# Three half blocks of the fifth strip taken ahead of the third strip's last part, in a gated SSM and MLP kernel

## The chip, the cores and the metric

The kernel runs on one core of a Trainium2 chip. The metric is device microseconds (us) of one execution, lower is better.

PE is TensorE (matmuls), PEld its weight loads, DVE is VectorE, ACT is ScalarE, SP issues most transfers. PSUM is the memory that takes PE's results, in banks. L267 is line 267 of the kernel; behind the edit the line numbers of the changed kernel are two higher. In views of the profile, `<-` in brackets names what ended an engine's wait, and "issue" is time in which the engine waited for nothing that the profile shows.

## The reference, cut to what matters

```python
x = A_x                                        # [1, 2048, 640]
g = sigmoid((x * gate_w).sum(-1, keepdims=True))
a = A_ref(x, ...)      # diagonal complex recurrence over 2048 tokens, 640 states
b = gelu(x @ w1 + b1) @ w2 + b2                # 640 -> 1728 -> 640, tanh gelu
return g * a + (1 - g) * b
```

The kernel takes the tokens in four chunks of 512. The change touches only the start: the first 768 columns of `x @ w1` for the first chunk.

## The kernel before

The first chunk's `x` comes as rows of tokens and is transposed on PE (a matmul with the identity, L233), one part of 128 tokens at a time, and copied from PSUM into `xT` by ACT or DVE. The 640 input columns are five blocks of 128 ("strips", `kd` = 0 to 4). Six banks of PSUM (`kf` = 0 to 5) collect `x @ w1` for six blocks of 128 output columns; all take their matmuls from line 267. The lines that matter, shortened:

```python
FA = 6; KD = 5; KA = 2; P = 128; CH = 512; HT = 256

def ff1_mm(p, c, kf, kd, t0=0, t1=CH, first=None, last=KD - 1):   # L267
    ...
    nc.tensor.matmul(p[:, t0:t1], lhsT=w, rhs=xT[c][:, kd, t0:t1], ...)

def strip(kd, t0, t1, first, f0=0, f1=FA):     # strip kd, tokens t0 to t1, for banks f0 to f1
    for kf in range(f0, f1):
        ff1_mm(banks[kf], 0, kf, kd, t0, t1, first, 3)

def part(kd, a):                               # one strip, 128 tokens: six matmuls of 128 columns
    strip(kd, a * P, (a + 1) * P, kd == 0)

def turn_rest(a, t, *parts):                   # transpose strips 2..4 of tokens part a into one bank t
    for k in range(KA, KD):
        turn(t, (k - KA) * P, a, k)            # L233
    for engine, k0, k1 in parts:               # copies out of that bank, in this order
        turned(engine, t, (k0 - KA) * P, a, k0, k1)   # DVE L240, ACT L242

# ... strips 0 and 1, the first parts turned ...
turn_rest(2, bank(), (nc.scalar, KA, KD))
part(2, 0)
nc.vector.tensor_tensor(out=u, ...)            # [128, 345] f32, for the sine tables (L381)
turn_rest(3, pA, (nc.scalar, KA + 1, KD), (nc.vector, KA, KA + 1))
...
part(2, 1)
part(2, 2)
part(2, 3)                                     # needs DVE's copy of turn_rest(3)
... # sine tables on ACT
for kf in range(FA):
    if kf == 3:
        nc.tensor.matmul(pA[:, 0:NB], lhsT=prmB[:], rhs=ident[:, 0:NB], ...)   # biases turned, L393
        ...
    for kd in (4, 3):
        ff1_mm(banks[kf], 0, kf, kd, 0, CH, False, 3)        # 512 columns
for kf in range(FA):
    ff1_act(banks[kf], 0, kf)                  # Gelu out of the banks, L272
# ... second group of w1 (w1b), third (w1c), then the recurrence's input (BT_re, L546) ...
```

Of the kernel before, what the change touches and what calls it, by code (L numbers as in the profile page):

```python
# [20 lines left out]
CH = 512  # L21
NCH = T // CH
KD = D // P
# [6 lines left out]
HT = H * P  # L30
# [11 lines left out]
def kernel(  # L42
# [32 lines left out]
    def bank(dtype=F32):  # L75
        return ps.tile([P, CH * 4 // (4 if dtype == F32 else 2)], dtype, name="bank")
# [140 lines left out]
    def pe(cols):  # L217
        ck.pe += cols / 2400.0 + 0.002
# [45 lines left out]
    def ff1_mm(p, c, kf, kd, t0=0, t1=CH, first=None, last=KD - 1):  # L264
        w, f0 = (w1a, 0) if kf < FA else (w1b, FA) if kf < FB else (w1c, FB)
        w = w[kd][:, (kf - f0) * P:(kf - f0 + 1) * P]
        nc.tensor.matmul(p[:, t0:t1], lhsT=w, rhs=xT[c][:, kd, t0:t1],  # L267
                         start=(kd == 0) if first is None else first, stop=(kd == last), skip_group_check=first is not None)
        pe(t1 - t0)
# [53 lines left out]
    banks = [bank() for _ in range(FA)]  # L323

    def strip(kd, t0, t1, first, f0=0, f1=FA):
        for kf in range(f0, f1):
            ff1_mm(banks[kf], 0, kf, kd, t0, t1, first, 3)
# [26 lines left out]
    def part(kd, a):  # L354
        strip(kd, a * P, (a + 1) * P, kd == 0)
# [28 lines left out]
    nc.vector.tensor_tensor(out=red, in0=u, in1=kk[:], op=ALU.subtract)  # L384
    part(2, 1)
    part(2, 2)
    part(2, 3)
    nc.scalar.activation(out=FSC[:, 0:KS, 0:NP], in_=red, func=ACT.Sin, scale=TWO_PI_M)
    nc.vector.scalar_tensor_tensor(out=ab, in0=red, scalar=-1.0, in1=red, op0=ALU.mult, op1=ALU.max)
    nc.scalar.activation(out=FSC[:, KS:2 * KS, 0:NP], in_=ab, func=ACT.Sin, scale=-TWO_PI_M, bias=halfpi[:])  # L390
    for kf in range(FA):
        if kf == 3:
            nc.tensor.matmul(pA[:, 0:NB], lhsT=prmB[:], rhs=ident[:, 0:NB], start=True, stop=True, skip_group_check=True)  # L393
            nc.vector.tensor_copy(out=colB[:], in_=pA[:, 0:NB])
            for j in range(KD):
                nc.vector.tensor_copy(out=w1c[j][:, n1c - 1:n1c], in_=pA[:, j:j + 1])
        for kd in (4, 3):
            ff1_mm(banks[kf], 0, kf, kd, 0, CH, False, 3)
    for kf in range(FA):
        ff1_act(banks[kf], 0, kf)  # L400
    two_banks = [bank(), bank()]
# [336 lines left out]
```

## Time and profile before

| | before |
|---|---|
| median of the first 3 runs | 215.99 us (215.34 to 216.0) |
| span of the profiled run | 213.7 us |
| PE busy | 210.0 us, 98% |
| DVE busy | 189.0 us, 88% |

From the profile's page: busy time, share of the span and instruction count of each engine, and the shares of the chain of work that ended last.

```profile
span 213.7 us, 3596 instructions
PE 210.0 (98%) x1407; PEld 126.1 (59%) x1407; DVE 189.0 (88%) x387; ACT 103.2 (48%) x186; POOL 1.0 (0%) x13
PE 98%; DVE 0%; ACT 0%; issue 0%
```

The kernel is bound by PE. A PE that is 98% busy is only improved by doing less on it or by closing what gaps are left. The chain of waits between 8 and 13 us shows one (start, length, what):

```profile
8.48 0.18 PE bank L233 x3
8.66 0.02 issue
8.68 0.39 ACT xT L242
9.08 0.02 issue
9.10 0.30 DVE xT L240
9.40 0.04 issue
9.45 1.79 PE bank L267 x12
```

The chain leaves PE after the three transpositions of the last 128 tokens, goes through a copy on ACT, then one on DVE, and comes back to PE at 9.45 us. The same stretch in order of time (start, length, engine, line, what, count, and in brackets the idle time before it with its releaser):

```profile
8.11 0.51 DVE L381 TENSOR_TENSOR gel<-tf,thp_c 128x345 f32<-128x345 f32 x1
8.32 0.33 PE L233 MATMUL bank<-ident,xn 128*128 128x128 bf16 x3
8.48 2.75 PE L267 MATMUL bank<-xT,w1a 128*128 128x128 bf16 x24
8.68 0.38 ACT L242 ACTIVATE xT<-bank 128x256 bf16<-128x256 f32 x1
9.10 0.29 DVE L240 CAST xT<-bank 128x128 bf16<-128x128 f32 x1 [0.48 <-ACT xT L242]
9.45 1.29 PEld L267 LDWEIGHTS <-w1a 128*128 128x128 bf16 x11 [0.25 <-issue]
11.07 0.17 PE L393 MATMUL bank<-ident,prmB 128*128 128x18 bf16 x1
11.31 0.18 DVE L394 COPY colB<-bank 128x18 f32<-128x18 f32 x1 [0.56 <-PE bank L393]
12.39 4.48 PE L267 MATMUL bank<-xT,w1b 128*128 128x512 bf16 x20
20.67 1.25 PE L546 MATMUL bank<-xT,BT_re 128*128 128x512 bf16 x5
```

The view merges matmuls and models their ends, so the gap is hidden in the line "8.48 2.75 ... x24"; only the weight loads show it (idle 0.25 before 9.45). Taken one by one, the trace's matmul starts are plain:

```
before: ... 8.987  9.043  9.098 | 9.446  9.501  9.556 ...
```

The spacing is 0.056 us except for one of 0.348: 0.29 us lost. DVE, which had to give PE the last copy, stood idle for 0.48 us waiting for ACT to finish its own copy out of the same PSUM bank.

### The profile page before, as it was taken

How to read it: one execution, taken by the hardware profiler on the slowest of the kernel's cores; microseconds unless marked ns; L12 is line 12 of the kernel's file. 1: busy time of each engine (PE TensorE's matmuls, PEld its weight loads, DVE VectorE, ACT ScalarE, POOL GpSimd, SP SyncE). 2: the span in 40 equal slices, each digit the busy share in tenths (PEclk: the TensorE clock that was granted, in tenths of full speed). 3: DMA queues.
4: the chain of work that ended last, by engine and by line, in shares of the span. 5: the costliest groups of instructions: out<-in, count | busy, mean ns of one | idle time of the engine just before them, and what ended most of it. 6: DMA issues, size and time to landing. Idle time of an engine off the chain costs nothing.

```text
span 213.7 us, 3596 instructions
## 1 busy us (share of the span) xinstructions
PE 210.0 (98%) x1407; PEld 126.1 (59%) x1407; DVE 189.0 (88%) x387; ACT 103.2 (48%) x186; POOL 1.0 (0%) x13
## 2 busy tenths in 40 slices
PE   8999999999999999999999999999999999999994
PEld 5845444454576644775457777444457687676773
DVE  2689999999998999999999999999999999993153
ACT  3699856675758588203563210455682422305100
POOL 1000000000000000000000000000000000000000
DMA  6859999998000000051000005100000000100011
GB/s 196 236 133 182 228 172 267 337 204 219 1 0 0 3 0 0 17 178 67 0 0 3 0 0 187 61 0 2 3 0 14 0 3 31 61 34 0 0 66 61
DMA packets 31571, 15.84 MB, mean 74 GB/s; under 512 B 22978, under 2 KB 31554, under 8 KB 31554
## 3 DMA queue, kind: packets, MB, share of 16 engines
q1 hardware_dynamic: 30850, 14.99, 28.8%
q10 hardware_dynamic: 704, 0.62, 0.9%
q8 instruction: 11, 0.18, 0.4%
q14 instruction: 6, 0.05, 0.1%
HBM read 7.48 MB, written 2.62 MB: 47 GB/s over the span
## 4 chain that ended last, share of the span: by engine, by line
PE 98%; DVE 0%; ACT 0%; issue 0%
PE bank L605 27%; PE bank L267 26%; PE bank L664 20%; PE bank L546 20%; PE bank L230 1%; PE bank L621 1%; PE bank L293 1%; PE bank L233 1%; ACT xT L242 0%; DVE ot L669 0%; PE bank L358 0%; DVE xT L240 0%; PE bank L283 0%; PE bank L393 0%; PE bank L368 0%
## 5 line engine op out<-in xcount | busy, mean ns | idle before, releaser
L605 PE MATMUL bank<-w_sb,gel 128*128 128x384 bf16 (+1 forms) x416 | 57.9, 299 | 0.0
L605 PEld LDWEIGHTS <-gel 128*128 128x128 bf16 x416 | 40.3, 98 | 17.0 <-issue 0.8
L549 ACT ACTIVATE bu<-bank 128x512 bf16<-128x512 f32 x40 | 23.6, 597 | 37.6 <-PE bank L546 37.6
L272 ACT ACTIVATE gel<-bank,colB 128x512 bf16<-128x512 f32 x52 | 33.9, 692 | 11.1 <-PE bank L267 10.8
L664 PEld LDWEIGHTS <-hs 128*128 128x128 bf16 x330 | 31.7, 98 | 11.6
L500 DVE TENSOR_TENSOR_SCAN g<-r_c,carry,v 128x512 bf16<-128x512 f32 x30 | 37.2, 1269 | 0.0
L613 ACT ACTIVATE gb<-bank,gcol 128x384 f32<-128x384 f32 (+1 forms) x32 | 15.1, 525 | 33.6 <-PE bank L605 16.8
L267 PE MATMUL bank<-xT,w1a 128*128 128x512 bf16 (+1 forms) x174 | 28.1, 315 | 0.1
L664 PE MATMUL bank<-CT_im,hs 128*128 128x320 bf16 (+2 forms) x165 | 27.1, 295 | 0.0
L664 PE MATMUL bank<-CT_re,hs 128*128 128x320 bf16 (+2 forms) x165 | 27.1, 295 | 0.0
L669 DVE SCALAR_TENSOR_TENSOR ot<-bank,gcol,gb 128x320 bf16<-128x320 f32 (+2 forms) x33 | 17.4, 533 | 9.9 <-PE bank L664 9.5
L546 PE MATMUL bank<-xT,BT_re 128*128 128x512 bf16 x100 | 24.8, 379 | 0.0
L546 PE MATMUL bank<-xT,BT_im 128*128 128x512 bf16 x100 | 24.8, 379 | 0.0
L267 PEld LDWEIGHTS <-w1a 128*128 128x128 bf16 x174 | 14.5, 99 | 11.8 <-issue 0.2
L267 PE MATMUL bank<-xT,w1b 128*128 128x512 bf16 x80 | 17.9, 379 | 0.0
L546 PEld LDWEIGHTS <-BT_im 128*128 128x128 bf16 x100 | 9.8, 98 | 11.8
L579 DVE TENSOR_TENSOR bank<-xn,Dbc 128x320 f32<-128x320 bf16 (+2 forms) x33 | 14.5, 481 | 2.3 <-ACT gb L613 2.3
L546 PEld LDWEIGHTS <-BT_re 128*128 128x128 bf16 x100 | 9.6, 98 | 11.0
L481 DVE TENSOR_TENSOR v<-wa,wb 128x512 bf16<-128x512 bf16 x40 | 15.2, 421 | 0.6
L594 ACT ACTIVATE bank<-b2bc 128x384 f32<-128x384 bf16 (+1 forms) x24 | 11.7, 524 | 7.3 <-DVE ot L669 7.3
L481 DVE TENSOR_TENSOR wa<-TCOS,g 128x1024 bf16<-128x1024 bf16 x20 | 13.7, 685 | 0.1
L267 PE MATMUL bank<-xT,w1c 128*128 128x512 bf16 x60 | 13.7, 379 | 0.0
(99 smaller groups left out, 166.1 us busy)
## 6 DMA issues: line engine op xcount, KB each, us to landing
out_dram<-ot SPq DMA_DIRECT2D x15, 160.0 KB, 1.8
w_sb<-in_B_w_dram SPq DMA_DIRECT2D x1, 2080.0 KB
xn<-in_A_x_dram SPq DMA_DIRECT2D x3, 640.0 KB
w1b<-in_B_w_dram SPq DMA_DIRECT2D x5, 128.0 KB, 4.2
w1c<-in_B_w_dram SPq DMA_DIRECT2D x5, 112.0 KB, 4.9
w1a<-in_B_w_dram ACTq DMA_DIRECT2D x2, 192.0 KB, 3.1
w1a<-in_B_w_dram SPq DMA_DIRECT2D x1, 384.0 KB, 3.4
xn<-in_A_x_dram SPq DMA_DIRECT2D x4, 64.0 KB, 3.2
```

What stands on the lines that cost most here:

```text
L267: nc.tensor.matmul(p[:, t0:t1], lhsT=w, rhs=xT[c][:, kd, t0:t1], start=(kd == 0) if first is None else first, stop=(kd == last), skip_grou ...
L272: nc.scalar.activation(out=gel[c][:, kf, :], in_=p[:, :], func=ACT.Gelu_apprx_tanh, bias=b1_c[:, kf:kf + 1])
L481: nc.vector.tensor_tensor(out=o, in0=a, in1=b, op=op)
L500: nc.vector.tensor_tensor_scan(s["g"][:, ri, :], r_c[:, ks:ks + 1].to_broadcast([P, CH]), s["v"][:, ri, :], init, ALU.mult, ALU.add)
L546: nc.tensor.matmul(p[:], lhsT=BT[ks >= KSA][:, kd, (ks % KSA if ks < KSA else ks - KSA) * P:][:, 0:P], rhs=xT[c][:, kd, :], start=(kd == 0 ...
L549: nc.scalar.activation(out=bu[:, ri, :], in_=p[:], func=ACT.Identity)
L579: dve_now(ck.pe, 0.45, lambda: nc.vector.tensor_tensor(out=p[:, 0:d1 - d0], in0=xn[c][:, a, d0:d1], in1=Dbc[:, d0:d1], op=ALU.mult))
L594: nc.scalar.activation(out=v, in_=src, func=ACT.Identity)
L605: nc.tensor.matmul(p[:, col:col + d1 - d0], lhsT=gel[c][:, kf, a * P:(a + 1) * P], rhs=w2_sb[:, kf, d0:d1], start=False, stop=False, skip_ ...
L613: nc.scalar.activation(out=gbs[ti][:, d0:d1], in_=p[:, col:col + d1 - d0], func=ACT.Identity, scale=gcol[:, 1, ti:ti + 1])
L664: nc.tensor.matmul(p[:, 0:d1 - d0], lhsT=hs[c][:, j, lo:lo + P], rhs=CT[:, j % KS, d0:d1], start=False, stop=(j == 2 * KS - 1), skip_group ...
L669: nc.vector.scalar_tensor_tensor(out=ot[:, d0:d1], in0=p[:, 0:d1 - d0], scalar=gcol[:, 0, ti:ti + 1], in1=gbs[ti][:, d0:d1], op0=ALU.mult, ...
```

## The change

The intent is to give PE something to do in the gap: half blocks (256 tokens) of the fifth strip whose operands are there already. What is taken ahead is then left out later.

```diff
     part(2, 1)
     part(2, 2)
+    AHEAD = 3
+    strip(KD - 1, 0, HT, False, 0, AHEAD)
     part(2, 3)
     ...
         for kd in (4, 3):
-            ff1_mm(banks[kf], 0, kf, kd, 0, CH, False, 3)
+            ff1_mm(banks[kf], 0, kf, kd, HT if kd == 4 and kf < AHEAD else 0, CH, False, 3)
```

Three matmuls of 256 columns are added, and three of 512 columns become 256.

## The prediction

> **What bounds the kernel now.** TensorE. The page's chain of waits that ended last is 98% PE, and the engine table gives PE 210.0 us busy of a 213.7 us span. I listed the start-to-start times of all 1407 matmuls: columns/2.4 GHz add up to 205.3 us and everything above that to 4.7 us, of which some 2.2 us lies before 5 us (half-speed matmuls at the start). After 5 us there is one real hole: the last matmul of the third strip's third part starts at 9.098 us, and the first of its last part at 9.446 us, where the spacing in that stretch is 0.056 us. That leaves 0.29 us of idle PE. The chain of waits shows the reason: issue 0.02, ACT xT 0.39, DVE xT 0.30, issue, and then the matmuls. The last part needs the third 128-row block of the first chunk's last 128 tokens; the copy of it on VectorE runs 9.10 to 9.39 us, after it waited 0.48 us for ScalarE's copy of the other two blocks. From 9.446 us to the end no gap between matmuls exceeds 0.1 us.
>
> **What the change does.** It puts three matmuls of 256 columns (fifth strip, kf 0 to 2, tokens 0 to 255) into that hole and makes three later 512-column matmuls 256 columns long. The number of columns is the same; three matmuls are added. "TensorE: Matmul & The Clock Gate" of the Trainium skill (section on 56 ns against 53.3 ns) gives N/2.4 GHz plus about 2.5 ns for each warm matmul; the trace agrees (216 ns at 512 columns, 56 at 128). So the addition costs about 3 x 2.5 = 8 ns, and three of 256 columns take about 0.33 us (estimate from those spacings). They fit the 0.29 us hole almost exactly: they would end near 9.48 us, just after the copy that opens the last part at 9.446 us.
>
> **Are the operands there?** Tokens 0 to 255 of the fifth block row are copied by ScalarE and VectorE before 8.2 us. The weights of the fourth and fifth strips are one transfer; its last piece lands at 8.39 us, 0.76 us before it is now needed at 9.15 us. So no new wait.
>
> **How much reaches the end.** All of it, about 0.29 us, if nothing behind is nearly late. PE moves up by 0.29 us, and VectorE too: its 0.56 us wait for the bias transpose (copy at 11.31 us) shrinks to about 0.27 us. ScalarE does not move (table load 11.38 to 12.66, first Gelu at 12.68 us), but banks come free long before they are refilled. The closest transfer is the fifth piece of the second group's w1: last packet at 13.59 us, needed near 14.12 us, after the change 13.83 us: 0.24 us are left. The imaginary-part weights of the recurrence land by 20.55 us for use at 21.75 us.
>
> **Prediction.** 215.99 - 0.29 = 215.7 us, a gain of 0.13%, below the spread of the runs of before (215.34 to 216.0). Range 215.1 to 216.2 us. Chances: faster by over 2% 0.01, within 2% 0.98, slower by over 2% 0.01.
>
> **What the profile would show.** A spacing of 0.06 to 0.11 us between all matmuls from 8.5 to 10 us; the bias transpose near 10.79 us instead of 11.07; the first matmul of the second w1 group near 12.1 instead of 12.39; the recurrence's first near 20.4 instead of 20.67; the span near 213.4 us.
>
> **What would make it wrong.** The weights land later in other runs, so that the three matmuls wait and push the last part back; the second group's transfer lands after 13.83 us, so that the gain is given back there; or PE, unseen in the trace, is met by a late bank or transfer later on.

## The result, and the profile after

| | before | after |
|---|---|---|
| median of 6 runs | 215.70 us (215.33 to 216.21) | 215.41 us (214.95 to 215.73) |
| ratio | | 0.9983, 95% interval 0.9962 to 1.0004 |
| span of the profiled run | 213.7 us | 213.8 us |

A ratio is worked out from the fast runs of both kernels of the same job, so it is not quite the ratio of the medians quoted. The interval includes 1: these six runs alone do not show a gain. The median lies inside the predicted range, but the span of the one profiled run did not get shorter, although 213.4 was predicted. That needs an explanation.

From the page after:

```profile
span 213.8 us, 3591 instructions
PE 209.5 (98%) x1399; PEld 126.2 (59%) x1410; DVE 189.2 (88%) x387; ACT 103.2 (48%) x186; POOL 1.0 (0%) x13
PE 95%; DMA 3%; SPq 0%; issue 0%; DVE 0%
```

There are 1410 weight loads, the three added ones included; that only 1399 matmuls are shown means that eleven records are missing, not that work is. The chain now starts with transfers (DMA 3%). Its part between 8 and 13 us:

```profile
4.59 3.56 DMA xn<-in_A_x_dram
8.16 0.05 issue
8.20 0.34 PE bank L233 x3
8.54 0.34 PE bank L267 x6
8.88 0.17 PE bank L233 x3
9.05 1.44 PE bank L267 x22
10.49 0.05 issue
```

The copies of ACT and DVE are gone from it: PE runs on from the transpositions into 22 matmuls. But it had waited for a transfer before that, up to 8.16 us. (The 0.05 "issue" at 10.49 stands where a 512-column matmul's record is missing.) In order of time, the lines that answer to those of before, and the wait that before had not:

```profile
6.92 0.17 PE L368 MATMUL bank<-ident,prmA 128*128 128x15 bf16 x1 [0.15 <-DMA prmA<-in_A_Lambda_re_dram]
8.72 0.33 PE L233 MATMUL bank<-ident,xn 128*128 128x128 bf16 x3
8.88 2.47 PE L267 MATMUL bank<-xT,w1a 128*128 128x128 bf16 x26
9.50 0.29 DVE L240 CAST xT<-bank 128x128 bf16<-128x128 f32 x1 [0.70 <-ACT xT L242]
11.19 0.17 PE L395 MATMUL bank<-ident,prmB 128*128 128x18 bf16 x1
11.43 0.18 DVE L396 COPY colB<-bank 128x18 f32<-128x18 f32 x1 [0.28 <-PE bank L395]
12.51 4.48 PE L267 MATMUL bank<-xT,w1b 128*128 128x512 bf16 x20
20.79 1.24 PE L548 MATMUL bank<-xT,BT_re 128*128 128x512 bf16 x4
```

And the single matmul starts (the three half blocks in brackets):

```
after:  ... 9.443  9.499 [9.555  9.664  9.773] 9.882  9.938 ...
```

Measured from the transpositions of the last 128 tokens (8.32 before, 8.72 after), everything behind comes sooner: the bias transposition after 2.47 instead of 2.75 us, DVE's wait for it is 0.28 instead of 0.56, the recurrence after 12.07 instead of 12.35. But those transpositions themselves came 0.40 us later. So one trace holds a gain of 0.28 and a loss of 0.40. The question is whether the loss belongs to the change.

To tell them apart I use one number per trace: the **stretch** from the start of the first of those three transpositions to the start of the kernel's last matmul. It is 202.408 us before (8.317 to 210.725) and 202.129 after (8.717 to 210.846). It leaves out the start, in which the transfers arrive. Behind that last matmul every trace has 2.94 to 2.96 us to its end, so what the stretch gains the span gains.

My theory (A): the gap is a fixed wait inside the kernel and the change closes it; nothing gives the gain back; and the start varies from run to run by itself. The rivals: the gap or the gain is luck of one trace; the change makes the start later; the gain comes from cutting the blocks and not from their place; or it is given back behind.

### The profile page after: what moved, and what is told of

Read it like the earlier page. It is cut to its first block, busy times and chain, and to the rows that moved or that the text cites. A ratio compares the mean times of both kernels' runs of the same rounds, so it can differ in the third digit from the quotient of the medians.

```text
span 213.8 us, 3591 instructions
## 1 busy us (share of the span) xinstructions
PE 209.5 (98%) x1399; PEld 126.2 (59%) x1410; DVE 189.2 (88%) x387; ACT 103.2 (48%) x186; POOL 1.0 (0%) x13
## 4 chain that ended last, share of the span: by engine, by line
PE 95%; DMA 3%; SPq 0%; issue 0%; DVE 0%
PE bank L607 27%; PE bank L267 25%; PE bank L666 20%; PE bank L548 20%; DMA xn<-in_A_x_dram 2%; DMA w1a<-in_B_w_dram 1%; PE bank L623 1%; PE bank L293 1%; SPq L130 0%; PE bank L233 0%; DVE ot L671 0%; PE bank L283 0%; PE bank L395 0%
## 5 line engine op out<-in xcount | busy, mean ns | idle before, releaser
L267 PE MATMUL bank<-xT,w1a 128*128 128x512 bf16 (+2 forms) x173 | 27.7, 310 | 0.2
```

## The experiments

Ten runs were made, all correct. This table holds what their traces and times gave, with before and after, twelve traces in all; "start" is the time of the first of the three transpositions. "Half speed" counts the matmuls of 128 columns between 3.9 and 6.5 us that were spaced about 0.107 us (0.097 to 0.108) instead of 0.056. (The one of ahead6 stands among fast ones and may be a wait.)

| run | start, us | half speed | stretch, us | ratio (95% interval) |
|---|---|---|---|---|
| before | 8.317 | 4 | 202.408 | |
| null | 8.689 | 14 | 202.406 | 0.9997 (0.9979 to 1.0015) |
| split_only | 9.095 | 14 | 202.419 | 1.0015 (0.9996 to 1.0035) |
| after | 8.717 | 2 | 202.129 | 0.9983 (0.9962 to 1.0004) |
| after2 | 8.766 | 16 | 202.123 | 0.9998 (0.9979 to 1.0016) |
| swapped | 8.320 | 0 | 202.122 | 0.9992 (0.9973 to 1.0011) |
| both | 8.762 | 17 | 202.128 | 0.9987 (0.9967 to 1.0006) |
| ahead6 | 8.326 | 1 | 202.135 | 0.9970 (0.9952 to 0.9988) |
| ahead6b | 9.070 | 23 | 202.135 | 0.9990 (0.9971 to 1.0009) |
| xearly | 8.434 | 10 | 202.123 | 0.9994 (0.9969 to 1.0019) |
| wide0 | 8.863 | 13 | 203.503 | 1.0045 (1.0021 to 1.0069) |
| wide12 | 8.050 | 0 | 202.365 | 0.9994 (0.9970 to 1.0017) |

### The kernel before against itself (null)

Edit: none.

> The kernel before, unchanged, against itself: a measure of the noise, and a second trace of it. Every theory: ratio 1.000 with an interval of some +-0.002. What it tells is where the start differs from trace to trace. Stretch from the first of the three transpositions of the last 128 tokens (8.317 us in the first trace of before) to the start of the last matmul (210.725): 202.41 us there. Theory A (the gap is a fixed wait inside the kernel, the start is what varies): this stretch repeats within 0.05 us and holds a gap of 0.29 us again, while the 8.317 us moves by some tenths. Rival B (the gap itself is luck of the first trace): the gap differs by more than 0.1 us.

Measured: 215.86 us against 215.85. The gap between matmuls is again 0.29 us (one spacing of 0.35 after 9.47 us), the stretch 202.406. The start is 8.689, 0.37 later than in the first trace, with the same kernel. So the gap is part of the kernel and not of one trace, and the start moves by tenths without any change. The interval of the times is +-0.0018, that is +-0.4 us: more than the gain that is looked for.

### The change again (after2)

Edit: none to the changed kernel.

> The changed kernel again, with more rounds. In the first trace of it the stretch from those transpositions to the last matmul was 202.13 us (8.717 to 210.846), 0.28 less than before, while its start came 0.40 us later. Theory A: stretch 202.13 again within 0.05, no gap before the third strip's last part, ratio 0.9987 (0.29 of 215.7) within its interval. Rival C (the change itself makes the start later, by 0.4 us, so that nothing is won): the transpositions start near 8.7 again, against 8.3 in the kernel before, and the ratio is 1.000.

Measured: stretch 202.123, no gap. The start is 8.766, near the 8.717 of the first trace of it. After two traces of each, the rival that the change itself delays the start (C) was still possible. The ratio is 0.9998, and its interval includes both the expected 0.9987 and 1.

### The same half blocks, but behind (split_only)

Against the kernel after:

```diff
-    AHEAD = 3
-    strip(KD - 1, 0, HT, False, 0, AHEAD)
     part(2, 3)
+    AHEAD = 3
+    strip(KD - 1, 0, HT, False, 0, AHEAD)
```

> The same three blocks cut in two, but the first halves taken after the third strip's last part instead of ahead of it: the same instructions in another order, the gap left open. Theory A: gap of 0.29 us there, stretch 202.42 us (before plus three matmuls' fixed cost, 0.008), ratio 1.000. Rival D (the cutting of the blocks, not their place, is what helps, by freeing something behind): stretch 202.13.

Measured: stretch 202.419, against 202.42 expected by A. The chain of waits of this run again goes through both copies:

```profile
9.46 0.39 ACT xT L242
...
9.88 0.30 DVE xT L240
...
10.22 0.93 PE bank L267 x10
```

So cutting the blocks wins nothing (D falls) and costs 0.011 us for three more matmuls; it is their place that matters. The start was 9.095, the latest of all: PE waited 0.50 us for a part of the input, in a kernel whose order up to there is that of before.

### The gap closed at its cause (swapped)

This is the kernel before, without any block taken ahead; only the order of two copies is turned round.

```diff
-    turn_rest(3, pA, (nc.scalar, KA + 1, KD), (nc.vector, KA, KA + 1))
+    turn_rest(3, pA, (nc.vector, KA, KA + 1), (nc.scalar, KA + 1, KD))
```

> The kernel before, with one change: of the two copies out of the last transposition's bank, the one on the vector engine (third block row) is written first and the one on the scalar engine second. If the vector engine's 0.48 us wait for the scalar engine is only the order of two readers of one bank, its copy then starts at once, about 0.45 us earlier, and ends before PE needs it. Theory A (this wait is the whole cause of the gap): the gap closes without any block taken ahead, stretch 202.12 us, 0.29 less than before, ratio 0.9987. Rival E (the vector engine is held by something else, the transposition or its own earlier work): the gap stays, or the scalar engine's copy, now 0.3 us later, opens a new one at the first block of the fifth strip (needed near 9.5 us).

Measured: stretch 202.122. In order of time:

```profile
8.32 0.33 PE L233 MATMUL bank<-ident,xn 128*128 128x128 bf16 x3
8.69 0.29 DVE L240 CAST xT<-bank 128x128 bf16<-128x128 f32 x1 [0.30 <-PE bank L233]
9.01 0.38 ACT L242 ACTIVATE xT<-bank 128x256 bf16<-128x256 f32 x1 [0.34 <-DVE xT L240]
10.79 0.17 PE L393 MATMUL bank<-ident,prmB 128*128 128x18 bf16 x1
12.11 0.59 PE L267 MATMUL bank<-xT,w1b 128*128 128x512 bf16 x2
```

DVE no longer waits for ACT; ACT now waits 0.34 us for DVE, and nobody waits for ACT (its copy ends at 9.40 us, 0.10 before PE's first matmul that needs it, at 9.49). The gap of PE is gone, without a matmul added. So the cause of the gap is the order of two readers of one bank. That they take turns is what the Trainium skill asks for ("PSUM — Partial Sum Buffer", section on bank collisions): two engines that read the same bank on the same partitions at the same time raise an error and mostly get wrong data, so every such pair must be put in order. The trace agrees as far as it shows a wait in either order (0.48 us of DVE, 0.34 of ACT); no run here lets the two overlap.

This trace happens to start at 8.320, as the first trace of before did, and it shows the very marks that the prediction had given for the change: 10.79 for the bias transposition, 12.11 for the second group (12.1 predicted), a span of 213.4 us.

### The two together (both)

Edit: the change, and the swapped order of copies.

> The change and the swapped copies together. Theory A (one gap of 0.29 us, which each of them closes by itself): no further gain; stretch from the first transposition of the last 128 tokens to the last matmul 202.13 us, as with either alone (202.12 to 202.13). Rival I (they act on different losses): stretch 201.84 us.

Measured: stretch 202.128. There is one loss of 0.28 us, and each of the two takes it away alone; they don't add.

### The gap made wider (wide0), and wider and filled (wide12)

```diff
+    for _ in range(4):
-    nc.vector.tensor_tensor(out=u, ...)
+        nc.vector.tensor_tensor(out=u, ...)
```

wide12 has this too, and twelve half blocks ahead:

```diff
+    AHEAD = FA
+    strip(KD - 1, 0, HT, False, 0, AHEAD)
+    strip(KD - 2, 0, HT, False, 0, AHEAD)
     part(2, 3)
     ...
-            ff1_mm(banks[kf], 0, kf, kd, 0, CH, False, 3)
+            ff1_mm(banks[kf], 0, kf, kd, HT, CH, False, 3)
```

> The kernel before with the gap made wider: the vector engine's product ahead of its last copy (0.51 us, next one 0.47 later) is done four times over instead of once (same values, right result). The last copy, so far 0.48 us idle before it, then comes about 3 x 0.47 - 0.48 = 0.93 us later, and the gap of 0.29 grows to about 1.2 us. Theory A: stretch to the last matmul 203.3 us, time +0.9 us against before, ratio 1.004. Rival F (a gap at the start is made up later, because PE meets other limits): the time moves by less than half of that.

> The same wider gap, and twelve half blocks (all six of the fifth strip and all six of the fourth, 256 tokens each) taken ahead of the third strip's last part: 12 x 0.109 = 1.31 us of work for a gap of 1.2 us. Theory A: no gap, stretch about 202.15 us (202.41 - 0.29 + 12 x 0.0025), 1.15 us less than wide0, ratio to before 0.999. Rival F: less than half of that difference to wide0. Rival G (what is gained is given back where the second group's w1 or a bank comes late): new gaps of together several tenths behind 12 us.

Measured, wide0:

```profile
8.66 2.18 DVE L382 TENSOR_TENSOR gel<-tf,thp_c 128x345 f32<-128x345 f32 x4
10.75 0.28 DVE L240 CAST xT<-bank 128x128 bf16<-128x128 f32 x1
...
11.09 1.79 PE L267 MATMUL bank<-xT,w1a 128*128 128x128 bf16 x12 [1.22 <-DVE xT L240]
```

The four products are spaced 0.55 us, not 0.47 as I had estimated, so the gap is 1.39 us (by the matmul starts) instead of 1.2. The stretch is longer than that of before by 1.095 us, and the gap by 1.09 (1.385 - 0.295). The time is longer by a ratio of 1.0045, about 0.97 us, with an interval that leaves 1 out. A gap at this place is paid in full at the end of the kernel (rival F falls).

In wide12 the half blocks bring the stretch back by 1.138 us (203.503 to 202.365), and the median from 217.06 to 216.12. But 202.15 was expected. The missing 0.22 us stands in two gaps: 0.07 us where 12 x 0.109 = 1.31 us did not quite fill a gap of 1.39, and 0.15 us at 14.24 us, where PE waits on the semaphore of ACT. There PE begins the ninth of its thirteen column blocks, and ACT has just ended its first Gelu:

```profile
13.50 4.73 ACT L272 ACTIVATE gel<-bank,colB 128x512 bf16<-128x512 f32 x8
```

(One Gelu takes 0.69 us, so the first ends at 14.19; the matmul that waited starts at 14.244.) That the wait is for the bank which this Gelu empties is read from the code and from this order of times; the record names only the semaphore. So rival G is right in kind for this kernel: when PE is moved up by more than a microsecond against ACT, it meets the Gelu that empties the first bank. The extra products themselves had put ACT back, so this limit is nearer here than in the change, where the first Gelu starts at 13.08 us and the ninth block at 14.67 (12.51 + 10 x 0.216).

### Six half blocks (ahead6, and again ahead6b)

Against the kernel after:

```diff
-    AHEAD = 3
+    AHEAD = FA
```

> The change with all six blocks of the fifth strip taken ahead instead of three: 0.65 us of work for a gap of 0.29. Theory A: the same gain as with three, less three matmuls' fixed cost, stretch 202.14 us; what is more than the gap is only moved. Rival H (the gain comes from the half blocks taken early, each worth 0.1 us): stretch 201.8 us.

> All six blocks taken ahead, once more. The first time its ratio was 0.997 with an interval that leaves out 1, although its stretch of 202.135 us was the same as with three blocks. Theory A: stretch 202.13 again, ratio 0.9987 within the interval, so that the 0.997 was the luck of the start. Rival H (six blocks win twice as much as three): ratio 0.997 again and stretch below 202.0.

Measured: stretch 202.135 both times, against 202.14 and 202.13 expected. What does not fit into the gap is only moved. The ratio of the first time, 0.9970, has an interval without 1, and taken alone it would pass for a gain of 0.3% over before. The second time it was 0.9990 with the same stretch. So rival H falls. That the first ratio was mostly the luck of the start is likely, as the two profiled runs start at 8.326 and 9.070 us, but the starts of the other runs were not recorded.

### An attempt at a better version (xearly)

```diff
     load_x0(nc.sync, 3, 4, 0, KA * P)
-    load_w1a(nc.sync, 2)
+    load_x0(nc.sync, H, TPC, KA * P, D)
     ...
     rows(nc.sync, prmA[2 * KS:3 * KS, :], A_Lambda_re)
-    load_x0(nc.sync, H, TPC, KA * P, D)
+    load_w1a(nc.sync, 2)
```

(on the kernel "swapped")

> An attempt at a better version: the swapped copies, and at the start the 192 KB of the input's last 256 tokens (later column blocks) issued before the third strip's weights instead of after them and three small rows; the weights, also 192 KB, take its place. In the traces so far PE waited 0.26 to 0.5 us for that part of the input in three of nine (landed 7.76 to 8.54 us), none in the others (6.94 to 8.15). Theory (the part lands about 1 us earlier and the weights are not needed before 8 us): no wait at the transpositions, the first of the last three at about 8.3 us or sooner if the clock is released early, stretch 202.12 us, time 0.1 to 0.2 us less on average than swapped, which five rounds can't tell from nothing. Rival: the weights are now late by as much, a gap at the third strip's first part.

Measured: stretch 202.123, no wait for a transfer at the start in this trace, and none for the third strip's weights. The ratio, 0.9994, tells nothing. A wait that shows in a part of the runs can't be judged by one trace without it, so whether this order is better stays open.

### What the start's variation is made of

The start lies between 8.05 and 9.10 us over twelve traces. The first cause is the number of half-speed matmuls. The same lines of two runs:

From swapped:

```profile
3.99 0.49 PE L267 MATMUL bank<-xT,w1a 128*128 128x128 bf16 x6
4.44 0.50 PE L267 MATMUL bank<-xT,w1a 128*128 128x128 bf16 x6
5.04 0.83 PE L267 MATMUL bank<-xT,w1a 128*128 128x128 bf16 x12
```

From ahead6b:

```profile
3.98 0.80 PE L267 MATMUL bank<-xT,w1a 128*128 128x128 bf16 x6
4.78 0.84 PE L267 MATMUL bank<-xT,w1a 128*128 128x128 bf16 x6
5.64 1.24 PE L267 MATMUL bank<-xT,w1a 128*128 128x128 bf16 x12
```

Both begin at the same time (3.99 and 3.98), and the third group begins 0.60 us later in ahead6b, whose matmuls are spaced 0.107 us until 6.4. The Trainium skill ("TensorE: Matmul & The Clock Gate", the section on the HAM clock gate) says that the array runs at half rate until it has been busy for a window of about 3.4 us, and that the window runs freely, so that the moment of release differs from run to run. The traces agree in part: the spacing is 0.107 or 0.056 us and little between, and the step came after 0 to 23 matmuls of the real work. But PE's first matmul starts at 0.77 us in all of them, and the step came 2.8 us later in ahead6, sooner than one such window, and 5.7 us later in ahead6b; the window itself is not seen in any trace. Each half-speed matmul costs 0.107 - 0.056 = 0.05 us, so 23 of them about 1.2 us. Between the starts of wide12 (no half-speed matmul, no late transfer) and ahead6b there are 1.02 us, because wide12 has one wait of 0.155 us (at 4.70 us) that ahead6b has not. The second cause is a late transfer: PE waited 0.25 us (after), 0.27 (swapped) and 0.50 (split_only) for the input's last 256 tokens, 0.32 (after) for the parameters, and 0.20 (ahead6) for an earlier piece of the input, all by the spacing of the matmul starts. Both appear in kernels with and without the change (late transfers in swapped, half speed in null), and after2, both and ahead6b have late starts without late transfers, while swapped and ahead6 start at 8.32 with the gap closed. The 0.40 us that the first trace of after had lost come from its two late transfers (0.32 and 0.25 us, partly set off by other waits of before), not from half speed, of which it had less than before; the 0.37 us of null come from half speed (14 such matmuls against 4). So the two losses are not of one kind, and the unchanged kernel's two traces hold no late transfer of this kind. But swapped has one without any added matmul, after2 has none with them, and the first edited instruction comes later: nothing ties the loss to the change.

### All times together

Over all jobs, the unchanged kernel was timed 45 times (mean 215.82 us, standard deviation 0.38), and the versions without the gap (after, after2, swapped, both, ahead6, ahead6b) 36 times (mean 215.52, standard deviation 0.32); xearly, whose start was rewritten, is left out. The difference is 0.30 us with a standard error of about 0.08 (0.38/sqrt(45) and 0.32/sqrt(36), added in squares). These are runs of several chips and rounds, so this is no paired ratio, but it agrees with the 0.28 us that the stretch gives.

## Why the prediction was right or wrong

- **PE bounds the kernel, and 0.29 us of idle PE before the third strip's last part is what the change can win: right.** The gap was 0.29 us in every trace with the old order (before, null, split_only), and a gap made wider by 1.09 us lengthened the stretch by 1.095.
- **Its reason, DVE's copy behind ACT's: right,** shown by swapped, which closes it by that order alone.
- **Three half blocks fit it almost exactly and cost about 8 ns: right.** They took 0.327 us (9.555 to 9.882). The fixed cost of three matmuls is 0.011 us in split_only.
- **The operands are there: right, with less in hand than stated.** The weights' last piece landed at 9.14 us in the trace after, for use at 9.555: 0.41 us, where 0.76 had been read from one trace.
- **All of it reaches the end: right.** Stretch shorter by 0.279 us (0.284 by the gap of 0.292 less 0.008), in after2 0.285. Behind 10.3 us, the matmul starts of before and after show the same eight spacings that are 0.09 to 0.1 us too long, and no other beside the missing records, so no new wait gives it back. DVE moved up with PE (its wait 0.28 us, 0.27 predicted), and ACT did not, as predicted (its first Gelu is 4.36 us behind the transpositions in both traces).
- **The time: right,** 215.41 us for 215.7 predicted, and 0.27 us by all 12 runs of the changed kernel (mean 215.55) against the 45 of before. The prediction took its 0.29 us off 215.99, the median of three runs; six runs gave 215.70. That the two medians differ by just the predicted 0.29 us is luck, as the interval of the ratio is +-0.45 us.
- **The marks in the profile (10.79, 12.1, 20.4 us, span 213.4): wrong in the trace after,** which has 11.19, 12.51, 20.79 and 213.8. This step failed because they were given as times from the span's start, taking the start of before's one trace as fixed. It varies by about 1 us. As differences to the transpositions they hold (2.47 us to the bias transposition; 10.79 - 8.32 = 2.47).
- **The risk that the second group's weights come late** did not occur. In the trace after they landed at 12.05 us for use at 14.24. What did come late, in wide12 only, was a bank.

## What to carry to other kernels

When a change is worth less than the spread of the times, measure it in the trace between two instructions that enclose it, and leave the start of the kernel out: here that stretch repeats within 0.01 us, where times differ by a microsecond. Before filling a wait with other work, ask what orders the two that wait on each other: turning round two readers of one PSUM bank gave the same gain with one line and no added matmul. A ratio whose interval just leaves out 1 is still to be repeated.

## What the Trainium skill lacked or had wrong

- "TensorE: Matmul & The Clock Gate", section "Back-to-back issue gap": it gives about 81 ns per matmul at 128 columns and 131 at 512 as the sustained rate of pairs of weight load and matmul. Here every matmul has its own weight load (1410 of them), and the spacing is 56 ns at 128 columns, 109 at 256 and 216 at 512, as its formula for an isolated gap has it.
- The same page says nothing of how the half rate looks in a profile's clock column: in ahead6b the granted clock reads 1.00 from 4 to 6 us while matmuls are spaced 0.107 us. Of the two, only the spacing shows it.
- "ScalarE: Activation LUTs", section "What ACT_TABLE_LOAD costs": it counts a drain of about 1.38 us on top of the load's 1.283. Here the load takes 1.283 us, but in before the copy ahead of it ends 0.02 us before it and the activation after it starts 0.01 us behind it (copy to 9.07, load from 9.09, sine at 10.38 us), with no such drain on either side.
- No page gives how far a kernel's start moves from run to run, late transfers included: 8.05 to 9.10 us at the same instruction over twelve traces. For its half-rate part alone "TensorE: Matmul & The Clock Gate", section on the HAM clock gate, has a transition about 4 us into the activity that varies by 0.5 us either way; here it came 2.8 (ahead6) to 5.7 us (ahead6b) after the first matmul.
